# Attention and a GELU MLP on one core: the last 64 tokens of every batch gathered into one chunk, and the first batch's work reordered

## The chip, the cores and the metric

The kernel runs on one core of one Trainium2 chip. The metric is device time in microseconds (us) of one execution. A profiled execution also gives a trace: when each instruction ran on TensorE (PE, with its weight loads as PEld), VectorE (DVE), ScalarE (ACT), GpSimd (POOL) and SyncE (SP), and when each DMA was issued and landed. ACT computes the exponentials and the GELUs, POOL and SP issue the DMAs, POOL through the software queue (q0, it can change types on the way), SP through the hardware queue (q1, it can transpose).

## What is computed

Attention with a forgetting factor over 8 batches of 8 heads, 576 tokens of 64 features; then a two-layer MLP with exact GELU on the 4,608 tokens of 512 features. All inputs and the output are float32.

```python
scores = scale * q @ k.T                       # per batch and head, 576 x 576
cum    = cumsum(log(clip(f, 1e-4, 1)))         # per batch and head
scores = where(causal, -1e9, scores + cum[i] - cum[j])
attn   = softmax(scores)
x      = (attn @ v) -> 4608 x 512              # heads side by side
out    = gelu(x @ w_in) @ w_out                # 512 -> 2048 -> 512
```

The factor exp(-cum[j]) is multiplied into v (and kept as a 65th column, which gives the softmax's denominator), and exp(cum[i]) cancels, so that the kernel exponentiates the bare scores.

## The kernel before

The work of one batch is *attention(b)* and then *gemm1(b)*; *gemm2(b - 1)* is spread as filler between the matmuls of attention(b). After the last batch come gemm2(7), gemm1(8) and gemm2(8) alone.

**Attention.** Heads go in four pairs, i = 0 to 3. For a pair, `scores` (L279) computes the transposed scores, keys by queries, in four PSUM tiles t = 0 to 3, whose make-up is the list `STILES` (L27): 512, 448, 512 and 192 columns per head. ACT exponentiates each tile (L294) into an `e` tile in bf16, and POOL zeroes the part above the diagonal with `affine_select` (L296), five times in a pair. The two heads of a pair use the one `kT` tile with two query tiles, `qA` and `qB`, whose other half is zero. `attend` (L308) multiplies `e` with the weighted v, `vw`, 15 matmuls of 65 columns a head; `normalize` (L323) divides by the 65th column on DVE. A pair's 576 tokens then go to `xT_sb`, transposed: for batch 0 by PE and a DVE copy (`to_xT`, L336), later by two DMA transposes on SP (`x_dma`, L344), one for tokens 0 to 511 and one for the last 64.

**The MLP.** `xT_sb` holds all 4,608 tokens in order, and is cut into nine chunks of 512, so that chunk c begins at token 512 c and a chunk crosses batches. `gemm1(c, ffb)` (L358) is four matmuls of 512 columns and a GELU on ACT, 16 of them a chunk; `gemm2(c)` (L376) is a generator of 64 matmuls of 512 columns, each 16 followed by a DVE copy and an output DMA on SP. `take` draws so many of them between the tiles of the scores, by the lists `FILL` and `FILL_1` (L469).

**The order** is written by hand (`manual_schedule`): each engine runs its instructions in the order of the program, and each tile pool hands out its buffers in turn. Pools that matter: `qk` with one buffer (the token-major q and k of one batch), `e` with three, `s_psum`, `o_psum` and `m_psum` with two each. `m_psum` serves gemm1 and gemm2, `s_psum` the scores and some transposes.

- Batch 0 (`first_attention`, L413) has no filler. Its q and k come in four loads of two heads; PE transposes them (`transposes_first`, L169) and DVE and ACT copy them out (L183). Scores of a pair come in twos between the transposes; both heads of a pair are attended at once (`attend_pair`); DVE weighs v for pairs 0 and 2 (L269, L449), POOL for pairs 1 and 3. The four loads of w_in are issued by POOL after the pair's third scores tile (L436).
- Gemm1(0) (L517 to 527) has the PE transposes of batch 1's pairs 0, 1 and 2 in `s_psum` after ffb 10, 13 and 15 (`transposes_pe`, L194; the 8 DVE copies of each are L222) and, after ffb 2, the four loads of w_out.
- Batch 1 transposes its pair 3 within attention (L486) and then loads batch 2's q and k (L487).
- From batch 2 on, q and k of the next batch are transposed by DMA, two heads at a time, eight DMAs a batch (`transpose_dma`, L229), and put into `qA`, `qB` and `kT` by eight DVE copies a pair (`untangle`, L243) during gemm1. SP's queue before an attention holds the five loads of the next batch's v (`load_v`, L103, called at L515), then, as the attention goes on, the DMA transposes, the output DMAs and `x_dma`.

The softmax here doesn't subtract the row's maximum and nothing guards it: scores larger than these inputs give would overflow.

## Time and profile before

| | us |
|---|---|
| median of 3 runs | 377.35 (374.38 to 379.9) |
| the profiled execution's own time | 375.81 |
| its span, from the first to the last instruction | 374.1 |
| PE busy | 342.8 |
| ACT busy | 214.0 |
| DVE busy | 171.5 |
| POOL busy | 131.1 |

The span is 1.7 us shorter than the profiled execution's time. A row of the profile gives the line in the kernel, the engine, the operation, the tiles (out<-in) and the shapes; "idle before" is the time that the engine stood still just before, with what released it. The row PEclk is the clock that TensorE was granted, in tenths of the full one. A busy PE is not PE at its peak, because matmuls overlap: a matmul of 512 columns is shown with 379 ns, but one starts every 216 ns.

### The profile page before, as it was taken

To read this page: it belongs to the slowest core of one execution; us is meant where nothing else is said; L and a number is where in the kernel's file an instruction comes from. 1 tells how busy PE (TensorE), PEld (TensorE's weight loads), DVE (VectorE), ACT (ScalarE), POOL (GpSimd) and SP (SyncE) were. 2 spreads that over 40 slices of the span, in tenths; PEclk is the share of its full clock that TensorE was granted. 3 is DMA by queue.
4 is the path that set the end of the run, shared out by engine and by line. 5 is a ranking of instruction groups with operands and counts; after the bars stand their busy time and mean duration, and the time that the engine had idled before them with its cause. 6 is when DMAs were issued, how large, how long until landed. Compare 5 with 4: busy or idle time off the path is not lost.

```text
span 374.1 us, 6875 instructions
## 1 busy us (share of the span) xinstructions
PE 342.8 (92%) x2665; PEld 185.4 (50%) x2665; DVE 171.5 (46%) x420; ACT 214.0 (57%) x293; POOL 131.1 (35%) x261
## 2 busy tenths in 40 slices
PE   2858949969999699999999999999999999999995
PEld 1545526624465245644564456445654565444442
DVE  6395385548034932477246723681459142011011
ACT  4656647506874378737872688179826882611610
POOL 6578236351155404470447044703560350000000
PEclk9999978999999999999999999999999999999999
DMA  7999999767986894459644976498540023002002
GB/s 110 181 204 184 196 212 162 107 131 138 212 146 87 144 219 109 100 126 210 137 100 119 193 120 106 132 193 140 108 117 2 28 50 102 0 30 84 0 30 84
DMA packets 111057, 45.37 MB, mean 121 GB/s; under 512 B 89968, under 2 KB 106352, under 8 KB 111024
## 3 DMA queue, kind: packets, MB, share of 16 engines
q1 hardware_dynamic: 94128, 31.30, 40.7%
q0 software_dynamic: 16896, 13.63, 24.2%
q8 instruction: 21, 0.34, 0.4%
q14 instruction: 12, 0.10, 0.1%
HBM read 37.90 MB, written 9.44 MB: 127 GB/s over the span
## 4 chain that ended last, share of the span: by engine, by line
PE 77%; ACT 8%; DVE 7%; DMA 3%; SPq 2%; issue 1%; DVEq 0%; ACTq 0%
PE ps L362 33%; PE ps L394 26%; PE s L284 10%; PE o L315 7%; ACT e L294 5%; DMA xT_sb<-x 3%; ACT L294 2%; DVE vw L269 1%; ACT g L374 1%; SPq L350 1%; DVE x L329 1%; DVE ot L403 1%; DMA f_sb<-in_f_dram 1%; SPq L404 1%; DVE qB L183 1%
## 5 line engine op out<-in xcount | busy, mean ns | idle before, releaser
L374 ACT ACTIVATE g<-ps 128x512 bf16<-128x512 f32 x144 | 86.0, 597 | 111.0 <-PE ps L362 111.0
L394 PE MATMUL ps<-w_out_sb,g 128*128 128x512 bf16 x576 | 144.7, 379 | 0.0
L362 PE MATMUL ps<-xT_sb,w_in_sb 128*128 128x512 bf16 x576 | 127.2, 379 | 7.9 <-DMA xT_sb<-x 7.9
L294 ACT ACTIVATE e<-s 128x1024 bf16<-128x1024 f32 (+2 forms) x128 | 103.5, 861 | 25.5 <-PE s L284 24.9
L296 POOL TENSOR_SCALAR_AFFINE_SELECT e<-e 128x256 bf16<-128x256 bf16 x160 | 62.5, 407 | 140.0 <-ACT e L294 138.8
L362 PEld LDWEIGHTS <-w_in_sb 128*128 128x128 bf16 x576 | 56.1, 98 | 76.5 <-issue 10.3
L403 DVE COPY ot<-ps 128x512 f32<-128x512 f32 x36 | 24.9, 692 | 125.7 <-PE ps L394 124.8
L394 PEld LDWEIGHTS <-g 128*128 128x128 bf16 x576 | 50.3, 98 | 41.0
L284 PE MATMUL s<-qA,kT 128*128 128x384 bf16 (+2 forms) x192 | 54.8, 293 | 9.6 <-ACT e L294 4.2
L284 PEld LDWEIGHTS <-kT 128*128 128x128 bf16 x384 | 37.6, 100 | 46.6 <-issue 11.9
L284 PE MATMUL s<-qB,kT 128*128 128x384 bf16 (+2 forms) x192 | 50.3, 294 | 0.3 <-DVE qB L183 0.3
L269 POOL TENSOR_TENSOR vw<-v,wT 128x640 bf16<-128x640 f32 x30 | 38.8, 1292 | 27.6 <-PE o L315 18.5
L315 PE MATMUL o<-vw,e 128*128 128x65 bf16 x960 | 43.6, 194 | 1.6 <-DVE vw L275 1.4
L315 PEld LDWEIGHTS <-e 128*128 128x128 bf16 x960 | 40.4, 98 | 9.1 <-issue 1.4
L328 DVE RECIPROCAL r<-o 128x5 f32<-128x5 f32 x64 | 12.4, 193 | 48.0 <-PE o L315 47.1
L252 DVE COPY kT<-tk 64x288 bf16<-64x288 bf16 x96 | 32.2, 336 | 1.4
L329 DVE TENSOR_TENSOR x<-o,r 128x320 bf16<-128x320 f32 x64 | 31.5, 492 | 2.2
L252 DVE COPY qA<-tq 64x288 bf16<-64x288 bf16 x48 | 20.8, 433 | 0.9
L252 DVE COPY qB<-tq 64x288 bf16<-64x288 bf16 x48 | 16.7, 348 | 0.7
L98 POOL DMA_DIRECT2D q<-in_q_dram x12 | 9.1, 756 | 9.0 <-DMA tq<-q 7.9
L294 ACT ACT_TABLE_LOAD x7 | 9.0, 1283 | 3.3 <-PE s L284 3.2
L374 ACT ACT_TABLE_LOAD x8 | 10.3, 1283 | 0.1
(52 smaller groups left out, 88.5 us busy)
## 6 DMA issues: line engine op xcount, KB each, us to landing
out_dram<-ot SPq DMA_DIRECT2D x36, 256.0 KB, 2.3
v<-in_v_dram SPq DMA_DIRECT2D x30, 256.0 KB, 9.3
q<-in_q_dram POOLq DMA_DIRECT2D x6, 576.0 KB, 7.5
k<-in_k_dram POOLq DMA_DIRECT2D x6, 576.0 KB, 10.7
v<-in_v_dram SPq DMA_DIRECT2D x20, 128.0 KB, 5.3
w_in_sb<-in_moe_w_in_dram POOLq DMA_DIRECT2D x4, 512.0 KB, 10.2
w_out_sb<-in_moe_w_out_dram POOLq DMA_DIRECT2D x4, 512.0 KB, 13.6
xT_sb<-x SPq DMA_TRANSPOSE x56, 2.4
```

What stands on the lines that cost most here:

```text
L252: nc.vector.tensor_copy(rows[:, odd], src[odd * D : (odd + 1) * D, 2 * i + h].rearrange("d j p -> d p j"),)
L269: eng.tensor_tensor(vw_of[b][:, hs, :, 0:D], v_of[b][:, hs, :, :], w.unsqueeze(3).to_broadcast([P, 2, NBLK, D]), Alu.mult,)
L284: nc.tensor.matmul(st[:, h, c : c + w], kT[i][:, K0[n] : K0[n] + P], qt[:, q0 : q0 + w], start=True, stop=True,)
L294: nc.scalar.activation(et[:, :, 0:c], st[:, :, 0:c], Act.Exp, scale=scale)
L296: nc.gpsimd.affine_select(out=et[:, :, c0 : c0 + P], in_=et[:, :, c0 : c0 + P], compare_op=Alu.is_ge, fill=0.0, base=0, pattern=[[0, 2], [ ...
L315: nc.tensor.matmul(o[:, m, :], e_of[b, i, t][:, h, c : c + P], vw_of[b][:, 2 * i + h, n, :], start=(n == 0), stop=(n == m),)
L328: nc.vector.reciprocal(r, o[:, :, D])
L329: nc.vector.tensor_tensor(x_of[b, i][:, :, h, :], o[:, :, 0:D], r.unsqueeze(2).to_broadcast([P, NBLK, D]), Alu.mult,)
L362: nc.tensor.matmul(ps, w_in_sb[:, kt, ffb * P : (ffb + 1) * P], xT_sb[:, kt, t0 : t0 + TC], start=(kt == 0), stop=(kt == n_dm - 1),)
L374: nc.scalar.activation(g_of[c][ffb], ps, Act.Gelu)
L394: nc.tensor.matmul(pss[ts], g_of[c][kt][:, ts * P : (ts + 1) * P], w_out_sb[:, kt, :], start=(kt == 0), stop=(kt == n_ff - 1),)
L403: nc.vector.tensor_copy(ot, pss[ts])
```

## The change

1. **Chunks.** Chunk b is now the first 512 tokens of batch b, and the ninth chunk is the last 64 tokens of all eight batches. `xT_sb` gives way to a tile `xT` a batch (two buffers) and a tile `tails`. `normalize` writes tokens 0 to 511 and the tail separately, one more small instruction a head (on ACT for pairs 2 and 3 of batch 0, else on DVE). `x_dma` is one DMA transpose a pair, and `x_tail_dma` one a batch, so that a batch has five in place of eight. The last 128 output rows of all are made in a part of 384 columns and one of 128.
2. **Transposes of q and k by DMA** take four heads each, four a batch in place of eight, in attention(b) at pair 0 and pair 1. The `qk` pool has two buffers.
3. **Loads of v** go into one fixed tile `v_sb`, the last block with 64 rows in place of 128; from batch 2 on they are issued within attention(b), after its second scores tile, behind two DMA transposes.
4. **Score tiles** are balanced: 448, 448, 448 and 320 columns per head. `e` has four buffers.
5. **Batch 0.** A matmul of the identity with a tile `after` (0 and -1e9) adds the mask in PSUM in place of POOL's `affine_select`. Scores of later pairs come ahead, and the heads of earlier pairs are attended between them. POOL weighs all four pairs of v. Two of the four copies to `xT` go to ACT. Nine matmuls on a zeroed tile (`warm_up`) come first, and four more after the first transposes. On POOL the loads of w_in, the weighing and the loads of batch 1 alternate; batch 1's v is loaded in there too.
6. **Batches 0 and 1.** The transposes of batch 1's pairs 0 and 1 come in gemm1(0) after ffb 6 and 8, those of pairs 2 and 3 in attention(1). The four loads of w_out and batch 2's q and k are issued before gemm1(0). v of batch 1 is weighed for pairs 0 and 1 after ffb 9 and 10, for pairs 2 and 3 in attention(1) at pair 2.
7. **Fillers at the end of an attention**: the lists end in 8, 0, 20 in place of 8, 4, 16, and 8, 0, 99 in place of 8, 4, 99.

```diff
 STILES = [
-    [(0, 0, 384), (4, 448, 128)],
+    [(0, 0, 256), (3, 384, 192)],
+    [(0, 256, 320), (4, 448, 128)],
     [(1, 128, 448)],
-    [(2, 256, 320), (0, 384, 192)],
-    [(3, 384, 192)],
+    [(2, 256, 320)],
 ]
...
-    qk_pool = ctx.enter_context(tc.tile_pool(name="qk", bufs=1))
+    qk_pool = ctx.enter_context(tc.tile_pool(name="qk", bufs=2))
-    e_pool = ctx.enter_context(tc.tile_pool(name="e", bufs=3))
+    e_pool = ctx.enter_context(tc.tile_pool(name="e", bufs=4))
+    xT_pool = ctx.enter_context(tc.tile_pool(name="xT", bufs=2))
...
+    def warm_up(n):
+        ps = m_psum.tile([P, TC], FP32, tag="m", name="ps_w")
+        for _ in range(n):
+            nc.tensor.matmul(ps, warm[:, 0:P], warm, start=True, stop=True)
...
-    def transpose_dma(b, i):
+    def transpose_dma(b, h0, h1):
...
     def scores(b, i, t):
...
-                    stop=True,
+                    stop=b > 0 or c not in SDIAG[t],
                 )
+            if b == 0 and c in SDIAG[t]:
+                for h in range(2):
+                    nc.tensor.matmul(
+                        st[:, h, c : c + P], ident_bf, after, start=False, stop=True
+                    )
...
-        for c0 in SDIAG[t]:
+        for c0 in SDIAG[t] if b else []:
...
     def normalize(b, i, h):
...
-            o[:, :, 0:D],
-            r.unsqueeze(2).to_broadcast([P, NBLK, D]),
+            o[:, 0:4, 0:D],
+            r[:, 0:4].unsqueeze(2).to_broadcast([P, NBLK - 1, D]),
...
+        tail = xt_of[b][D:P, i, h, :], o[D:P, 4, 0:D]
+        if b == 0 and i > 1:
+            nc.scalar.mul(*tail, r[D:P, 4:5])
+        else:
+            nc.vector.tensor_scalar(*tail, r[D:P, 4:5], None, Alu.mult)
...
     def x_dma(b, i):
-        x, q0 = x_of[b, i], b * S
         nc.sync.dma_start_transpose(
-            xT_sb[:, i, q0 : q0 + 512].rearrange("d (m p) -> d m p", p=P),
-            x[:, 0:4].rearrange("p m h d -> p (m h d)"),
+            xT(b)[:, i, :].rearrange("d (m p) -> d m p", p=P),
+            x_of[b, i].rearrange("p m h d -> p (m h d)"),
         )
+
+    def x_tail_dma(b):
         nc.sync.dma_start_transpose(
-            xT_sb[:, i, q0 + 512 : q0 + S].unsqueeze(1),
-            x[D:P, 4].rearrange("p h d -> p (h d)"),
+            tails[:, :, b * TL : (b + 1) * TL],
+            xt_of[b][D:P].rearrange("p i h d -> p (i h d)"),
         )
...
     def gemm1(c, ffb):
-        t0 = c * TC
+        src = xT(c) if c < B else tails
...
     def first_attention():
...
+        warm_up(9)
         transposes(0, o_psum, "o")
+        zero_halves(range(2, HP))
+        warm_up(4)
         scores(0, 0, 0)
+        transposes(1, m_psum, "m")
         scores(0, 0, 1)
...
+        scores(0, 1, 3)
+        weigh_v(0, 0)
+        load_w_in(0)
+        load_w_in(1)
+        weigh_v(0, 1)
+        load_qk_tokens(1, 0, 4)
+        weigh_v(0, 2)
+        weigh_v(0, 3)
+        load_w_in(2)
+        load_w_in(3)
+        nc.gpsimd.memset(v_sb[:, :, 0, 0:1], 0.0)
+        load_v(1, 0, 4)
+        load_v(1, 4, 8)
+        load_qk_tokens(1, 4, 8)
         scores(0, 2, 0)
+        attend_head(0, 0)
         scores(0, 2, 1)
+        attend_head(0, 1)
         scores(0, 2, 2)
         scores(0, 2, 3)
+        attend_head(1, 0)
         scores(0, 3, 0)
+        attend_head(1, 1)
+        to_xT(0, 0, nc.vector.tensor_copy)
         scores(0, 3, 1)
         scores(0, 3, 2)
+        attend_head(2, 0)
         scores(0, 3, 3)
+        attend_head(2, 1)
+        to_xT(0, 1, nc.scalar.copy)
+        attend_head(3, 0)
+        attend_head(3, 1)
+        to_xT(0, 2, nc.scalar.copy)
+        to_xT(0, 3, nc.vector.tensor_copy)
...
-    FILL = [[4, 6, 2, 2], [2, 2, 2, 2], [2, 2, 2, 2], [2, 2, 1, 1], [8, 4, 16]]
-    FILL_1 = [[0, 0, 0, 0], [2, 2, 2, 2], [2, 2, 2, 2], [2, 2, 2, 2], [8, 4, 99]]
+    FILL = [[4, 6, 2, 2], [2, 2, 2, 2], [2, 2, 2, 2], [2, 2, 1, 1], [8, 0, 20]]
+    FILL_1 = [[0, 0, 0, 0], [2, 2, 2, 2], [2, 2, 2, 2], [2, 2, 2, 2], [8, 0, 99]]
...
     def attention(b, fill, counts):
...
-                if b == 1 and i == 0 and t == 2:
-                    transposes_pe(1, 3, in_s=False)
-                    load_qk_tokens(2)
...
+                if t == 0 and b > 1 and i < 2:
+                    transpose_dma(b + 1, 4 * i, 4 * i + 4)
+                if t == 1 and i == 0 and b > 1:
+                    load_v(b + 1)
+                if b == 1 and (i, t) in ((0, 0), (0, 3)):
+                    transposes_pe(1, 2 + t // 3, o_psum)
+                if b == 1 and i == 2 and t in (0, 2):
+                    weigh_v(1, 2 + t // 2)
                 take(fill, counts[i][t])
...
         x_dma(b, i)
+        x_tail_dma(b)
         if b == 1:
-            transpose_dma(2, 3)
+            transpose_dma(2, 0, 4)
+            transpose_dma(2, 4, 8)
+            load_v(2)
         take(fill, 999)
 
     for b in range(B):
         if b == 0:
             first_attention()
-            load_v(1, 0, 4)
-            load_v(1, 4, 8)
         else:
-            load_v(b + 1)
             attention(b, gemm2(b - 1, b == 1), FILL_1 if b == 1 else FILL)
+        if b == 0:
+            for c in range(4):
+                load_w_out(c)
+            load_qk_tokens(2)
+            x_tail_dma(0)
         for ffb in range(n_ff):
             gemm1(b, ffb)
...
+            if b == 0:
+                if ffb in (6, 8):
+                    transposes_pe(1, ffb // 2 - 3, s_psum)
+                if ffb in (9, 10):
+                    weigh_v(1, ffb - 9)
...
+                if ffb == 14:
+                    load_qk_tokens(b + 2)
```

## The prediction

> **What bounds the kernel now.** I read the page's busy rows and slices first, then the table of stretches, the chain of waits, and the timelines of ACT, PE and SP where the table shows idle PE.
>
> ```profile
> PE 342.8 (92%) x2665; PEld 185.4 (50%) x2665; DVE 171.5 (46%) x420; ACT 214.0 (57%) x293; POOL 131.1 (35%) x261
> PE   2858949969999699999999999999999999999995
> PEclk9999978999999999999999999999999999999999
> ```
>
> PE bounds the kernel: from slice 8 on it hardly stops. What can be won is its idle time, 31.3 us, and that lies mostly in the first 125 us. Table of stretches (length; busy time of PE, PEld, DVE, ACT, POOL; clock, DMA):
>
> ```profile
> 0.00:33.40 33.40, 20.07 (x290) 14.66 (x291) 23.77 (x47) 19.45 (x23) 23.47 (x49) 1.00 0.98 167
> 33.40:51.50 18.10, 15.45 (x102) 7.75 (x101) 8.19 (x18) 9.55 (x16) 9.01 (x13) 1.00 1.25 197
> 51.50:84.80 33.30, 27.17 (x248) 16.07 (x249) 19.23 (x48) 15.74 (x18) 14.94 (x30) 0.90 0.83 143
> 98.70:125.70 27.00, 23.79 (x231) 13.94 (x229) 11.20 (x26) 15.48 (x19) 15.03 (x30) 1.00 0.77 135
> 139.70:163.00 23.30, 23.11 (x229) 13.83 (x228) 7.63 (x20) 15.43 (x18) 11.39 (x25) 1.00 0.51 108
> 328.80:370.40 41.60, 41.55 (x193) 18.55 (x190) 4.85 (x8) 10.15 (x17) 0.00 (x0) 1.00 0.12 45
> ```
>
> The reader sees PE idle 13.3 us in batch 0's attention, 2.7 about gemm1(0), 6.1 in batch 1, 3.2 in batch 2, and almost nothing in an undisturbed batch. In the first stretch ACT is the longest dependent chain, and it waits for scores between its bursts:
>
> ```profile
> 9.78 1.83 ACT L294 ACTIVATE e<-s 128x1024 bf16<-128x1024 f32 x2 [2.15 <-PE s L284]
> 24.17 1.41 ACT L294 ACTIVATE e<-s 128x1024 bf16<-128x1024 f32 x2 [2.28 <-PE s L284]
> 27.20 3.17 ACT L294 ACTIVATE e<-s 128x1024 bf16<-128x1024 f32 x4 [1.63 <-PE s L284]
> ```
>
> Next, PE waits for DVE's copies after gemm1(0), and for the DMA of x after attention(1), while SP has worked without a break since 62.81:
>
> ```profile
> 51.47 0.34 PE L284 MATMUL s<-qA,kT 128*128 128x384 bf16 x1 [2.65 <-DVE kT L222]
> 80.36 0.81 PE L362 MATMUL ps<-xT_sb,w_in_sb 128*128 128x512 bf16 x3
> 84.77 1.46 PE L362 MATMUL ps<-xT_sb,w_in_sb 128*128 128x512 bf16 x6 [3.60 <-DMA xT_sb<-x]
> ```
>
> ```profile
> 78.35 1.27 SPq L238 DMA_TRANSPOSE tq<-q  x1
> 79.67 1.27 SPq L238 DMA_TRANSPOSE tk<-k  x1
> 81.04 1.00 SPq L404 DMA_DIRECT2D out_dram<-ot  x2
> 82.13 1.22 SPq L346 DMA_TRANSPOSE xT_sb<-x  x1
> ```
>
> Measured from GELU end to GELU end in the chain, batches 2 to 6 take 40.9, 37.7, 38.3, 38.5 and 37.7 us. 37.65 is the undisturbed period.
>
> **What stays.** The number and columns of the gemm matmuls (nine chunks) and of the scores (1,664 a head and pair) are the same, so the period of 37.65 and the last 41.5 us of matmuls (328.84 to 370.37) stay. ACT's work a pair too: 2 x 1.02 + 0.91 + 0.49 = 3.44 us before, 3 x 0.91 + 0.70 (320 columns, between the rows of 0.49 and 0.91) after. The tail's multiply (eight a batch, 0.23 each by DVE's 64x64 copy) lies under PE, since DVE has 7 to 12 us of work in a 23 us attention; without that cover it would cost 1.8 a batch.
>
> **Step 1, batch 0 (gemm1(0) begins at 33.4).** DVE now copies kT before it zeroes the other halves, so qB is out at 7.9 in place of 9.0; 13 warm-up matmuls (0.43 each at half clock) fill PE from 1.4 to 5.3, before k lands at 5.58, and to 7.8 or 8.7. The first exponential begins at 8.9 (8.5 to 10.0). All 16 are 13.8 us. Mask matmuls: 40 of 128 columns at 0.055 to 0.11, 2.2 to 4.4 us of PE beside ACT. They free POOL of 20 selects (0.41 each, 8.1 us), and DVE loses two weighings (1.95 + 0.73 each). POOL now weighs all four: the first when v has landed (15.2, as before), 1.5 each (1.29 + 0.22), with four DMA issues of 0.75 between: 15.2, 18.2, 21.2, 22.7, done at 24.2. Pair 1 attended at 19.7 holds the next scores back some 0.5, and the second and third scores tiles behind transposes cost ACT 0.8 more. ACT also gets two multiplies (0.25 each) and ends at 24.6; then two heads (0.47 each), normalize (0.20 + 0.41, twice), four transposes and the copy (0.35 + 0.45): gemm1(0) at 27.2. Low end, no hole in ACT: 25.5. High end: POOL's small cast took 0.84 and 0.82 beside DVE's weighing, 0.22 to 0.28 otherwise; I take 0.22, since DVE's weighing is gone, but with 0.84 four times and a cold PE it is 30. **Minus 6.2 (minus 7.9 to minus 3.4).**
>
> w_in must land by then: before, its four loads took 15 us from first issue to last landing. Now two are issued at 16.7, landing at 22 to 24; batch 1's q and k (first half) by 27, the other two by 34, due at 27.2 + 7 and + 10.4. Covered, by little for the third.
>
> **Step 2, gemm1(0).** 16 x 0.867 + 2 x 0.51 for transposes = 14.9, against 18.07 to the first scores at 51.47: one group of transposes fewer, and the copies (3.9 us a pair) of both done before the end. **Minus 3.2.** If they were not, the 2.65 returns.
>
> **Step 3, attention(1).** Before 28.9 (51.47 to 80.36), of which 6.9 until the first filler. New is that pairs 2 and 3 are transposed here in `o_psum`, whose two buffers wait for DVE: pair 3's k cannot start before 5 us, so the next scores come at 5.4 and ACT idles 0.7. Then PE has three pairs of scores, eight heads and 64 fillers, 22.2 us: 27.6. Bounds: 25 (only PE's work, 23.8, and the table load of 1.28), 31.5 (v of batch 1, issued at 25 beside the weight loads. There q1 moved 0.04 MB/us before; 1.2 MB then land at about 54, and POOL wants them at 53). **Minus 1.3 (minus 3.9 to plus 2.6).**
>
> **Step 4, x of batch 1.** SP had 8 transposes of q and k and 8 of x before the gemm, about 1.27 and 1.23 each. Now the q and k transposes stand behind x, and x needs one DMA. From the last head: 0.65 + 1.23 + 1.2 to land = 3.1, under 32 fillers of 0.216 (6.9). **Minus 3.6.**
>
> **Step 5, batch 2.** Queue: v(2) now stands behind batch 2's transposes and is issued as gemm1(1) begins; it lands 8.2 later, POOL weighs for 6 us, and only then issues q and k of batch 3, whose loads take 6.0 and 9.3. SP meets their transposes first in attention(2): it waits till 10.4 us into it, then v (4.8), two transposes, outputs and four of x: the last lands at 26.3, where PE is ready at 23.75 and has 0.65 of work without it. Stall 1.9 to 2.5 in place of 3.3. **Minus 0.9 (minus 3.3 to plus 1.5).**
>
> **Step 6, batches 3 to 7.** SP had 8 x 1.27 + 8 x 1.23 + 4 x 0.52 + 10.4 to 12.4 (v) = 32.5 to 34.5 us of work in 37.65; that lateness is the 0.6 and 0.9 lost in batches 4 and 5. Now 4 x 1.3 + 5 x 1.23 + 2.1 + 4.8 to 12.4 = 18 to 26. A transpose of one block took 1.22 and of six 1.27, so I take 1.3 for twelve; its bound is 2.5. v is issued when no q and k load runs (alone: 4.8 on SP). 20 fillers (4.3) cover the last x's 3.1. **Minus 1.5 (to plus 6).**
>
> **Step 7, end.** The last copy is 128 columns: 0.25 for 0.69, and its DMA 64 KB for 256; 16 matmuls more cost 0.05. **Minus 0.5 (minus 0.8 to plus 0.3).**
>
> Sum: 6.2 + 3.2 + 1.3 + 3.6 + 0.9 + 1.5 + 0.5 = 17.2; span 356.9, profiled time 358.6. The profiled execution stood 1.5 under the median of the runs, so the median: **360**.
>
> **The clock.** In the trace, matmuls of 448 columns start 0.37 apart at 9.54 and 0.19 apart at 19.86: half clock first, full from about 17.7. It fell again from 52.05 to 58.88 (the 0.90 above), after PE had idled 2.65. I take full clock from about 7. The Trainium skill, "TensorE: Matmul & The Clock Gate", Part 1, says that one busy window of about 3.4 us lifts the gate, which the warm-up would meet. Its Part 4 says transposes do not count as busy in the same way, which speaks against the change: with 24 transposes between the warm-ups the clock would rise only with the scores. By Part 1 the sum stands; by Part 4 it is 1.2 us more. No run here separates them.
>
> **The rivals.**
> *Loads collide in the first 60 us.* For it: DMA is already near its limit there (0.98 and 1.25 of share), and POOL's queue mixes weighing with issuing. Against it: no more bytes, and none due earlier than my landings. Steps 1 and 3 then give back 5: 365.
> *The clock does not hold.* Cold batch 0 (the first two tiles of scores and a group of transposes at half speed: 0.6 + 0.5 + 0.5, less 0.4 under ACT: 1.2) and a half clock in attention(1), where fillers are still 0 for a pair (7 us at half speed, half of it behind ACT, 3.4): 364.6.
> *SP becomes the bound: slower.* v now stands ahead of x within an attention. If its issue takes 12.4 us there as well, and twelve blocks take 2.5: q and k transposes until 3.3, v 15.7, two more 20.7, outputs 1.0 and x 4.9: 26.6, landed at 27.9, against 24.4 needed: 3.4 in each of six batches, less the 2.3 already counted in batch 2: plus 18, 378. It decides from 2.9 us a batch. Against it: v alone took 4.8.
> *Fewer stalls still* (batch 2 none, ACT without holes): 356.
>
> **How the numbers follow.** My forecast 0.60 (own range 357 to 363), loads 0.14, clock 0.10, fewer stalls 0.11, SP 0.05. The range 354 to 368 leaves out SP and the worst of the loads. A measurement here tells about 2%, 7.5 us, from no change: faster is below 369.8. All but SP and a part of the loads (0.04, with more than 5 given back) lie there: 0.91; same 0.07, which takes that part and 0.03 of SP's 0.05; slower 0.02, where SP costs 4.2 a batch or more.
>
> **What would show it.** Gemm1(0)'s first matmul at 27 with ACT's exponentials nearly unbroken from 9; first scores of batch 1 some 15 us later without a wait on a copy; no wait on the DMA of x after attention(1), one of about 2 after attention(2), none later; periods of 37.65; v's five issues in 5 us of SP. Wrong if PE's idle time returns at the start of batch 1, if x is waited for in every batch, or if the period itself grows.

## The result and the profile after

The changed kernel takes 389.77 us (median of 4 runs, 388.09 to 391.0), the kernel before beside it 376.42 (374.38 to 379.9). The ratio is 1.034, with a 95% interval of 1.025 to 1.043: slower by 3.4%, where 360.0 was forecast. The profiled execution took 390.52, its span 388.8. The four executions span 386.4 to 389.3, so that spans less than about 3 us apart say little by themselves, and the stages are read instead.

The page of the changed kernel shows PE busier than before only in sum; three dips stand out: in slices 6 and 12 (counted from 0) and at the end.

```profile
PE 346.9 (89%) x2684; PEld 189.4 (49%) x2730; DVE 177.4 (46%) x478; ACT 216.9 (56%) x298; POOL 124.9 (32%) x248
...
PE   7989795999981799999999999999999999999940
...
PEclk9999998999997599999999999999999999999985
```

The table of stretches of the changed kernel, cut where its stages begin (length; busy time and count of PE, PEld, DVE, ACT, POOL; granted clock, DMA share, GB/s):

```profile
0.00:27.40 27.40, 22.67 (x339) 16.20 (x340) 21.14 (x49) 20.23 (x28) 19.94 (x39) 1.00 1.00 158
27.40:42.40 15.00, 14.87 (x87) 7.25 (x89) 7.67 (x16) 10.17 (x16) 3.05 (x4) 1.00 1.23 193
42.40:77.00 34.60, 26.91 (x252) 16.15 (x256) 16.95 (x43) 16.35 (x19) 13.01 (x28) 0.95 0.86 133
...
115.40:128.40 13.00, 1.42 (x4) 0.43 (x5) 9.98 (x29) 0.00 (x0) 5.83 (x10) 0.70 0.97 171
128.40:144.50 16.10, 16.05 (x61) 6.72 (x62) 3.35 (x11) 8.96 (x15) 0.00 (x0) 0.81 0.98 190
144.50:331.60 187.10, 185.62 (x1454) 102.63 (x1481) 94.52 (x268) 125.89 (x170) 67.07 (x138) 1.00 0.53 102
...
373.90:388.80 14.90, 0.00 (x0) 0.00 (x0) 0.03 (x1) 0.00 (x0) 0.00 (x0) 0.59 0.12 45
```

The first two rows and the long row of batches 3 to 7 are as good as forecast or better. The third has 7.7 us of idle PE, the fourth 11.6 of 13, and in the last no engine works for 14.9 us, while DMA moves 45 GB/s at a share of 0.12, about 2 of 16 engines.

Set side by side, with each stage from the end of the one above, that is from the end of its last matmul or of the wait behind it (us; "fixed" is the version of the experiments in which three costs are taken away):

| stage | before | forecast | changed | fixed |
|---|---|---|---|---|
| to the first matmul of gemm1(0) | 33.3 | 27.2 | 27.4 | 27.6 |
| gemm1(0), with the wait behind it | 18.1 | 14.9 | 15.2 | 15.2 |
| attention(1) | 28.9 | 27.6 | 34.5 | 29.9 |
| gemm1(1), attention(2), gemm1(2) | 58.7 | 54.2 | 67.6 | 51.4 |
| batches 3 to 7 | 189.8 | 188.3 | 187.1 | 187.1 |
| from there to the end | 45.3 | 44.8 | 57.1 | 46.7 |
| span | 374.1 | 356.9 | 388.8 | 357.9 |

So 31.9 us are missing against the forecast. They lie in three places, 6.9 in attention(1), 13.4 about batch 2 and 12.3 at the end; the other stages together are 0.7 better than forecast.

**Attention(1) and batch 2.** PE's timeline in the changed kernel (start, length; in brackets the idle time before and who ended it):

```profile
60.84 0.22 PE L343 MATMUL o<-vw,e 128*128 128x65 bf16 x2 [2.50 <-POOL vw L298]
61.53 0.27 PE L343 MATMUL o<-vw,e 128*128 128x65 bf16 x3 [0.47 <-POOL e L324]
63.27 0.24 PE L343 MATMUL o<-vw,e 128*128 128x65 bf16 x1 [1.48 <-POOL e L324]
...
120.44 0.79 PE L403 MATMUL ps<-xT,w_in_sb 128*128 128x512 bf16 x2 [5.06 <-DVE ot L450]
122.29 0.59 PE L403 MATMUL ps<-xT,w_in_sb 128*128 128x512 bf16 x1 [1.06 <-DMA xT<-x]
128.36 16.28 PE L403 MATMUL ps<-xT,w_in_sb 128*128 128x512 bf16 x60 [5.48 <-DMA xT<-x]
```

In attention(1) PE waits for POOL, which weighs v and has its selects queued behind that. In batch 2 it waits three times at the head of gemm1(2), and when it goes on at 128.4 the clock is half until 134.4: 60 matmuls take 16.28. The releaser of the first of these waits, an output copy of DVE, is itself held: DVE stood 7.1 us before it, in `normalize`, for a buffer of x that a DMA had still to read. POOL's timeline names what it waited for itself:

```profile
59.34 1.28 POOL L292 TENSOR_TENSOR vw<-v_sb,wT 128x640 bf16<-128x640 f32 x1 [4.05 <-DMA v_sb<-in_v_dram]
...
60.71 0.77 POOL L324 TENSOR_SCALAR_AFFINE_SELECT e<-e 128x256 bf16<-128x256 bf16 x2
...
88.78 1.28 POOL L292 TENSOR_TENSOR vw<-v_sb,wT 128x640 bf16<-128x640 f32 x1 [20.89 <-DMA v_sb<-in_v_dram]
...
94.26 0.81 POOL L102 DMA_DIRECT2D q<-in_q_dram  x1
95.07 0.77 POOL L102 DMA_DIRECT2D k<-in_k_dram  x1
```

Both times it is v. The second time the loads of batch 3's q and k stand behind the weighing. SP's timeline shows what follows from that, queue entry after queue entry (start, time to issue):

```profile
103.67 2.43 SPq L262 DMA_TRANSPOSE tk<-k  x1
106.20 4.35 SPq L114 DMA_DIRECT2D v_sb<-in_v_dram  x5
110.59 2.28 SPq L262 DMA_TRANSPOSE tq<-q  x1
112.91 1.37 SPq L262 DMA_TRANSPOSE tk<-k  x1
...
115.40 2.53 SPq L385 DMA_TRANSPOSE xT<-x  x2
...
118.66 3.46 SPq L385 DMA_TRANSPOSE xT<-x  x2
```

SP could not pass `tk<-k` before k landed, and everything else of attention(2) stood behind it, x last. The chain of waits has the flights themselves (start and length):

```profile
44.71 14.46 DMA v_sb<-in_v_dram
...
84.23 4.38 DMA v_sb<-in_v_dram
...
115.40 2.43 DMA xT<-x
120.41 7.91 DMA xT<-x
```

Two transposes of x, 512 tokens of one pair each: one lands 2.43 after its issue, the other 7.91. The second was issued 0.8 us after POOL had issued the load of batch 4's q (119.65, landing at 126.95). The experiments are about these three places, and about what the right parts of the forecast rest on.

### The profile page after: what moved, and what is told of

Same layout as the page of the kernel before. It is cut to its first block, busy times and chain, and to the rows that moved or that the text cites. A ratio compares the mean times of both kernels' runs of the same rounds, so it can differ in the third digit from the quotient of the medians.

```text
span 388.8 us, 6967 instructions
## 1 busy us (share of the span) xinstructions
PE 346.9 (89%) x2684; PEld 189.4 (49%) x2730; DVE 177.4 (46%) x478; ACT 216.9 (56%) x298; POOL 124.9 (32%) x248
## 4 chain that ended last, share of the span: by engine, by line
PE 66%; SPq 12%; DMA 8%; POOL 6%; issue 2%; DVE 1%; ACT 0%; POOLq 0%; DVEq 0%; ACTq 0%
PE ps L441 26%; PE ps L403 26%; SPq L114 9%; PE s L307 8%; DMA v_sb<-in_v_dram 6%; PE o L343 6%; POOL vw L292 3%; DMA xT<-x 3%; SPq L262 3%; POOL k L102 1%; POOL e L324 1%; POOL q L102 1%; DVE x L359 0%; POOL w_in_sb L160 0%; DVE ot L450 0%
## 5 line engine op out<-in xcount | busy, mean ns | idle before, releaser
L441 PE MATMUL ps<-w_out_sb,g 128*128 128x512 bf16 (+2 forms) x557 | 138.7, 374 | 1.6
L403 PE MATMUL ps<-xT,w_in_sb 128*128 128x512 bf16 x503 | 115.9, 387 | 12.7 <-DMA xT<-x 6.5
L322 ACT ACTIVATE e<-s 128x896 bf16<-128x896 f32 (+1 forms) x128 | 104.8, 863 | 24.2 <-PE s L307 17.7
L450 DVE COPY ot<-ps 128x512 f32<-128x512 f32 (+2 forms) x37 | 25.0, 677 | 121.6 <-PE ps L441 121.4
L441 PEld LDWEIGHTS <-g 128*128 128x128 bf16 x592 | 52.4, 98 | 42.5
L292 POOL TENSOR_TENSOR vw<-v_sb,wT 128x640 bf16<-128x640 f32 x32 | 40.8, 1276 | 55.1 <-DMA v_sb<-in_v_dram 46.2
L307 PE MATMUL s<-qA,kT 128*128 128x256 bf16 (+2 forms) x192 | 51.8, 282 | 2.7 <-ACT e L322 2.4
L307 PE MATMUL s<-qB,kT 128*128 128x256 bf16 (+2 forms) x192 | 48.5, 282 | 0.5 <-DVE qB L206 0.5
L359 DVE TENSOR_TENSOR x<-o,r 128x256 bf16<-128x256 f32 x64 | 27.2, 425 | 9.3 <-DMA xT<-x 7.1
L369 DVE TENSOR_SCALAR xt<-o,r 64x64 bf16<-64x64 f32 x60 | 17.5, 291 | 1.4
L403 PE MATMUL ps<-tails,w_in_sb 128*128 128x512 bf16 x62 | 14.2, 378 | 0.1
```

The costliest lines, as they stand in the source:

```text
L292: nc.gpsimd.tensor_tensor(vw_of[b][:, hs, :, 0:D], v_sb[:, hs, :, :], w.unsqueeze(3).to_broadcast([P, 2, NBLK, D]), Alu.mult,)
L307: nc.tensor.matmul(st[:, h, c : c + w], kT[i][:, K0[n] : K0[n] + P], qt[:, q0 : q0 + w], start=True, stop=b > 0 or c not in SDIAG[t],)
L322: nc.scalar.activation(et[:, :, 0:c], st[:, :, 0:c], Act.Exp, scale=scale)
L359: nc.vector.tensor_tensor(x_of[b, i][:, :, h, :], o[:, 0:4, 0:D], r[:, 0:4].unsqueeze(2).to_broadcast([P, NBLK - 1, D]), Alu.mult,)
L403: nc.tensor.matmul(ps, w_in_sb[:, kt, ffb * P : (ffb + 1) * P], src[:, kt, :], start=(kt == 0), stop=(kt == n_dm - 1),)
L441: nc.tensor.matmul(pss[ts][:, c0:c1], g_of[c][kt][:, ts * P : (ts + 1) * P], w_out_sb[:, kt, c0:c1], start=(kt == 0), stop=(kt == n_ff - 1),)
```

## The experiments

Spans are compared, one execution each, unless a ratio is given.

**The end: one output DMA a batch** (`tail_by_batch`). The rows of the last chunk belong to two batches of 64 in each 128. The changed kernel writes them as one DMA of shape 2x64x512.

```diff
-                    rows = out.rearrange("(b s) d -> b s d", s=S)[
-                        n * ts : n * (ts + 1), TC:S, c0:c1
-                    ]
+                    for j in range(P // TL):
+                        r0 = (P // TL * ts + j) * S + TC
+                        nc.sync.dma_start(
+                            out[r0 : r0 + TL, c0:c1], ot[j * TL : (j + 1) * TL, c0:c1]
+                        )
+                    yield
+                    continue
```

> Each output DMA of the last chunk (two batches of 64 rows, 2x64x512) is cut into two of 64 rows, one a batch; the last 128 rows stay cut into 384 and 128 columns. Theory A, a DMA whose outermost dimension is 2 runs on two of the 16 DMA engines: after the last matmul the changed kernel needed 15.2 us, with a DMA share of 0.12, that is 2 of 16. With 64 rows outermost the end comes 3 to 4 us after the last matmul, and the span falls by 11 to 12 us, from 388.8 to 377. Rival B, the short rows of the column parts (1,536 and 512 bytes) are what is slow: they are unchanged here, so the span stays at 387 to 389. Rival C, the number of stores in the queue: there are more of them, so it stays or grows.

Span 376.2, 12.6 less. The stretch from the last matmul to the end, in this kernel:

```profile
371.40:376.20 4.80, 0.01 (x1) 0.00 (x0) 0.29 (x1) 0.00 (x0) 0.00 (x0) 1.00 0.22 55
```

4.8 us in place of 15.2. The other 2.2 of the difference lie in attention(1) (0.8 shorter) and batch 2 (1.4), which this edit doesn't touch.

**The end: no split of columns** (`tail_whole_cols`), with the output still written as 2x64x512.

```diff
-        if c == B:
-            order[-n_ff:] = [
-                (n_sub - 1, kt, part)
-                for part in ((0, 3 * P), (3 * P, d_model))
-                for kt in range(n_ff)
-            ]
```

> The last 128 rows are made whole, 512 columns and one DMA; the DMAs of the last chunk keep the two batches outermost. Theory A (two engines): the bytes and the engines are as before, so the end comes as late, span 388 to 390. Rival B (short rows): 10 us less, 378.

The end takes 15.0 us after the last matmul, again at a share of 0.12. So the shape of the DMA is the cost, and the split in columns neither costs nor brings anything that can be seen there. The span is 385.2, 3.6 less and under the 388 to 390 expected, but not at the end: attention(1) took 31.5 in place of 34.5 and batch 2 1.6 less, while gemm1(0) began 1.2 later. The edit touches none of these, so two executions can differ by that much there.

**Batch 2: the load of q and k earlier** (`qk3_early`): the load of batch 3's q and k at ffb 0 of gemm1(1), ahead of the weighing, in place of ffb 14.

```diff
+                if b == 1 and ffb == 0:
+                    load_qk_tokens(3)
...
-                if ffb == 14:
+                if ffb == 14 and b > 1:
```

> In gemm1(1) POOL issues the loads of batch 3's q and k before it weighs batch 2's v, not after. Theory: batch 2's stall of 13 us before gemm1(2) (115.4 to 128.4) comes from POOL waiting until 88.6 for v, so that k of batch 3 landed at 103.6, and SP, whose queue has its transpose first, fell 10 us behind; x of the last pair was then issued at 120.4, into the loads of batch 4, and landed 7.9 us later. With the loads out by 78 the transposes run when attention(2) begins; gemm1(2) follows without a stall over 1 us, the half clock of 120.7 to 134.4 is gone, and the span falls by 13 to 15 us, to 374 to 376. Rival: the transposes of twelve blocks (2.3 us on SP at 110.6 and 199) and the new place of v keep SP late whatever k does: a stall of 5 us or more stays.

From the end of gemm1(1) to gemm1(2) it is 23.4 us in place of 29.4, and gemm1(2) takes 14.0 at full clock in place of 24.2: batch 2's stall is gone. But gemm1(1) now takes 20.3 in place of 14.0. POOL had nothing to do and issued the loads at 66.9, still within attention(1). PE's timeline:

```profile
75.93 0.81 PE L403 MATMUL ps<-xT,w_in_sb 128*128 128x512 bf16 x3
80.20 16.01 PE L403 MATMUL ps<-xT,w_in_sb 128*128 128x512 bf16 x61 [3.46 <-DMA xT<-x]
```

and the flight that it waited for, in the chain of waits:

```profile
70.47 9.70 DMA xT<-x
```

The stall has moved to the x of batch 1: span 377.8, 10.9 less, of which 16 come from batch 2 and 6 are given back here; 374 to 376 was expected.

**Attention(1): a second tile for v** (`v1_second_tile`), so that batch 1's v needn't wait for the weighing of batch 0's, and is issued right after the first two loads of w_in.

```diff
-    v_sb = consts.tile([P, H, NBLK, D], FP32)
+    v_sb = [consts.tile([P, H, NBLK, D], FP32, name=f"v_sb{i}") for i in range(2)]
...
         load_w_in(1)
+        nc.gpsimd.memset(v_sb[1][:, :, 0, 0:1], 0.0)
+        load_v(1, 0, 4)
+        load_v(1, 4, 8)
         weigh_v(0, 1)
...
```

> v has two tiles in turn, and batch 1's v is issued by SP after the first two loads of w_in (about 17.5 us) in place of 24.7, since it need not wait for batch 0's weighing. Theory: attention(1)'s 34.6 us against 27.6 forecast come from the second half of batch 1's v, which landed at 59.2 behind the loads of weights, while POOL's selects queue behind the weighing. Landed by 50, attention(1) takes 27.5 to 29 us and the span falls by 6 to 7, to 382 to 383; gemm1(0) may lose up to 1.5 where w_in lands later. Rival: the wait for o_psum and the copies of pairs 2 and 3, and the half clock from 62.7, set attention(1): it stays above 32 us.

The rows of gemm1(0) and attention(1):

```profile
27.60:44.30 16.70, 16.69 (x90) 7.86 (x90) 7.69 (x16) 10.22 (x16) 5.99 (x9) 0.90 1.24 195
44.30:73.40 29.10, 26.48 (x257) 16.25 (x256) 16.93 (x43) 16.46 (x19) 10.51 (x24) 0.94 0.90 147
```

Attention(1) takes 29.1 in place of 34.5, and no PE instruction waits for a weighing. The span falls by 3.7, not the 6 to 7 expected, because gemm1(0) had 3.4 us of half clock (0.90 in its row) and cost 1.5 more. Why the clock fell there is open; in the 3.4 us before it PE was busy for 1.8.

**The three together** (`all_fixed`): the second tile for v, the output by batches (both edits as above), and the load of batch 3's q and k behind the last weighing of attention(1), where v is there already.

```diff
                 if b == 1 and i == 2 and t in (0, 2):
                     weigh_v(1, 2 + t // 2)
+                    if t == 2:
+                        load_qk_tokens(3)
...
-                if ffb == 14:
+                if ffb == 14 and b > 1:
```

> The changed kernel with the three named costs taken away together: v of batch 1 goes to a second tile and is issued before the scores of batch 0's second half; the last rows go out as one DMA of 64 rows a batch; the load of batch 3's q and k is issued in attention(1), after the last weighing, and no longer in gemm1(1). Theory (three separate costs, each a transfer): attention(1) takes 29 us in place of 34.65, gemm1(1) stays at 14, gemm1(2) follows 23 to 24 us after the end of gemm1(1) and runs at full clock, the last output lands 4.8 us after the last matmul; span 388.8 less 10.4 (end), less 4 to 6 (attention(1), after the 1.5 that gemm1(0) gives back), less 13 to 15 (batch 2): 358 to 362, time 360 to 364, under the kernel before by 3 to 4%. Rival (the loads of batch 3 only collide elsewhere, as they did with x when they were issued at the start of gemm1(1)): the DMA of x after attention(1) lands some 8 us late and gemm1(1) takes 20 again; span 365 to 368. Rival (the costs are not independent; DMA traffic of the first 120 us is simply too much for the time it has): span 370 or more.

359.66 us (median of 4 runs), the kernel before beside it 377.23: a ratio of 0.954, 95% interval 0.950 to 0.958. The span is 357.9, just under the 358 to 362 expected. Its table from attention(1) on:

```profile
42.80:72.70 29.90, 24.73 (x251) 15.30 (x255) 16.93 (x43) 16.36 (x19) 12.04 (x26) 1.00 1.25 193
72.70:86.70 14.00, 13.95 (x66) 6.39 (x66) 11.10 (x33) 8.96 (x15) 2.35 (x3) 1.00 1.08 204
86.70:110.10 23.40, 23.13 (x229) 14.16 (x232) 9.36 (x27) 16.23 (x19) 15.19 (x32) 1.00 0.74 139
110.10:124.10 14.00, 13.95 (x66) 6.36 (x66) 11.85 (x33) 8.96 (x15) 3.21 (x6) 1.00 0.80 145
124.10:311.20 187.10, 185.61 (x1454) 102.63 (x1480) 94.48 (x268) 125.91 (x170) 67.19 (x138) 1.00 0.59 113
311.20:353.10 41.90, 41.68 (x205) 19.48 (x206) 5.40 (x8) 10.16 (x17) 0.00 (x0) 1.00 0.15 44
353.10:357.90 4.80, 0.00 (x0) 0.00 (x0) 0.29 (x1) 0.00 (x0) 0.00 (x0) 0.77 0.23 55
```

The three costs were independent enough to be taken away together: no stretch after attention(1) has more than 0.3 us of idle PE till the last matmul but for the 1.5 in the five batches. The clock is full from 4.1 until after the last matmul. This version is faster than both kernels. Attention(1) still has one wait of 2.3, for a select that stands on POOL behind the weighing and, from 58.27 to 59.85, behind the issuing of batch 3's q and k.

**The late flight by itself** (`qk4_late`). The changed kernel, in which POOL copies one element of gemm1(2)'s first output before it loads batch 4's q and k, so that this load can't fly beside x.

```diff
+    probe = consts.tile([P, 1], BF16)
...
                 if ffb == 14:
+                    if b == 2:
+                        nc.gpsimd.tensor_copy(probe, g_of[b][0][:, 0:1])
                     load_qk_tokens(b + 2)
```

> The changed kernel, but the load of batch 4's q and k waits (one element copied by POOL) for the first GELU of gemm1(2), so that it can't be in flight beside x of batch 2. Theory (a DMA transpose that meets a load of q and k in flight lands some 6 to 8 us late): the fourth transpose of x, issued at 120.4 as before, lands at 122 to 123 in place of 128.3, the next 5.5 us of idle PE and most of the half clock that follows are gone, and gemm1(2) ends at 137 to 139 in place of 144.6; the 5.06 us before gemm1(2) stay, since they come from x being issued late. Span 381 to 383. Rival (the fourth transpose is late for what stands ahead of it on SP's own queue, the five loads of v and the output): it still lands at about 128 and the span stays 387 to 389.

The chain of waits and PE's timeline of this kernel:

```profile
122.63 2.65 DMA xT<-x
```

```profile
122.61 1.00 PE L404 MATMUL ps<-xT,w_in_sb 128*128 128x512 bf16 x2 [4.84 <-DVE ot L451]
124.48 0.58 PE L404 MATMUL ps<-xT,w_in_sb 128*128 128x512 bf16 x1 [0.88 <-DMA xT<-x]
125.33 15.36 PE L404 MATMUL ps<-xT,w_in_sb 128*128 128x512 bf16 x61 [0.26 <-DMA xT<-x]
```

The same transpose behind the same queue flies 2.65 us in place of 7.91; the wait of 5.48 becomes 0.26, and the wait of 5 before it stays. The rival (SP's own queue ahead of it) is out. The sizes are smaller than I expected: the span is 384.8, 4.0 less, not 6 to 8. From its first matmul on gemm1(2) takes 6.1 less (18.1 for 24.2). But gemm1(0) began 1.2 later in this run, x was issued 2.2 later, and after 4.84 us of idle PE the clock was halved all the same, for 6.8 us in place of 13.7.

**Transposes of two heads** (`two_head_transposes`): eight DMAs a batch for q and k in place of four.

```diff
-        for src, dst in zip(qk_of[b], tq_of[b]):
-            nc.sync.dma_start_transpose(
-                dst[:, h0:h1].rearrange("d h j p -> d (h j) p"),
-                src[:, h0:h1].rearrange("p h c -> p (h c)"),
-            )
+        for g in range(h0, h1, 2):
+            for src, dst in zip(qk_of[b], tq_of[b]):
+                nc.sync.dma_start_transpose(
+                    dst[:, g : g + 2].rearrange("d h j p -> d (h j) p"),
+                    src[:, g : g + 2].rearrange("p h c -> p (h c)"),
+                )
```

> The changed kernel with the DMA transposes of q and k of two heads each, as before: eight a batch, at the same places. SP then has some 4 x 1.27 = 5 us more to issue in a batch. Theory (SP has room once v takes 4.8 and x five DMAs): batches 3 to 7 keep their period, 37.4 to 37.6, and batch 2 is as late as in the changed kernel or up to 3 us later; span 388 to 393. Rival (the four-head transposes are what gained the 0.25 us a batch, or SP is near its limit): period 38 or more, span 392 to 400.

Span 398.1, 9.4 more. Batches 3 to 7 keep 187.1 us exactly, so SP is no bound there. Batch 2 is 8 us later, where I had expected 3 at most: v of batch 2 stands behind eight transposes and is weighed from 93.38 on, then the loads (98.87) and all that SP has behind them move along, and x meets batch 4's load again. Its last flight in the chain of waits:

```profile
128.14 10.88 DMA xT<-x
```

So here fewer transposes helped where SP was late, in batch 2, and nowhere else. The span lies in the rival's range, but not for the rival's reason, since the period is unchanged.

**No warm-up** (`no_warm_up`): the changed kernel without the 9 + 4 matmuls on zeros.

```diff
-        warm_up(9)
...
-        warm_up(4)
```

> The changed kernel without its 13 warm-up matmuls. If they are what lifted the clock at 4.7 us, the first group of transposes and the first scores run at half clock, full clock comes some 7 us or more after 4.7, and gemm1(0) begins 0.6 to 1.2 us later than 27.4, at 28.0 to 28.6. If ACT's chain covers it, the clock rises late but gemm1(0) still begins at 27.4 to 27.6. If the transposes lift the clock as well as matmuls do, full clock comes within 3.4 to 6.8 us of the first transpose (5.6), by 12.4 at the latest.

The clock was full from 16.2 us, not 4.7, and gemm1(0) began at 31.06: 3.7 us later, three times what I had put on it. The second q and k also landed 1.7 us later than in the changed kernel (10.01 for 8.34), so not all of the 3.7 need be the clock. But the span is 387.5, which is 1.3 *less* and within the spread of the changed kernel. The table from the first transpose on:

```profile
5.80:10.60 4.80, 3.38 (x44) 2.67 (x46) 3.00 (x7) 2.35 (x4) 2.48 (x8) 1.00 1.18 174
10.60:16.20 5.60, 5.60 (x61) 3.96 (x57) 3.19 (x6) 2.61 (x4) 0.80 (x1) 1.00 0.91 188
...
46.20:76.90 30.70, 26.33 (x252) 16.31 (x255) 16.94 (x43) 16.46 (x19) 13.35 (x28) 0.94 0.89 134
```

(The clock column doesn't show the cold start as less than 1.00; that the clock was half is read from the matmuls: a transpose group of ten takes 0.70 in place of 0.47.) Attention(1) takes 30.7 in place of 34.5: it ends at 76.9 for 77.0, though gemm1(0) ended at 46.2 for 42.5. In the seven kernels here that keep v of batch 1 in the one tile it ended at 75.2 to 77.8, in no order with the end of gemm1(0). In all seven POOL waited for v before it weighed pair 2 of batch 1, at 58.9 to 60.6; in the four kernels with the second tile it did not wait there, and weighed at 54.8 to 57.0. What batch 0 won, attention(1) gave back.

**The three together, no warm-up** (`fixed_no_warm_up`), the same two lines taken out of `all_fixed`.

> The kernel with the three costs taken away, without its 13 warm-up matmuls. In the changed kernel they moved gemm1(0) by 3.7 us but the span by 1.3. Theory (there attention(1) waited for v of batch 1, which lands at the same time either way, and gave back the rest): with v in a second tile more of the 3.7 reaches the end: gemm1(0) at 31.0 to 31.4, span 360.4 to 361.6 (357.9 + 2.5 to 3.7). Rival (what follows batch 0 is limited by the transfers of w_in, w_out and of q and k here too): span 358.5 to 359.5.

Gemm1(0) begins at 29.81, 2.2 later than with the warm-up, less than the 3.4 to 3.8 that I expected, and gemm1(1) (74.95 for 72.74), every later stage and the end (360.1 for 357.9) are 2.2 later too. So here all of it reaches the end, which is the theory; the size between the two ranges comes from the smaller shift at the start. Here full clock came at 13.8, and the second q and k landed as with the warm-up (8.62).

**The old score tiles** (`old_tiles`): `all_fixed` with the lists `STILES` and `SDIAG` of before (`SDIAG` names where the diagonal lies in each tile).

```diff
 STILES = [
-    [(0, 0, 256), (3, 384, 192)],
-    [(0, 256, 320), (4, 448, 128)],
-    [(1, 128, 448)],
-    [(2, 256, 320)],
+    [(0, 0, 384), (4, 448, 128)],
+    [(1, 128, 448)],
+    [(2, 256, 320), (0, 384, 192)],
+    [(3, 384, 192)],
 ]
...
```

> The kernel with the three costs taken away, with the score tiles of before (512, 448, 512 and 192 columns per head in place of 448, 448, 448 and 320). Batches 3 to 7 took 37.42 us with the new tiles; before with only the chunks changed 37.67. Theory (the balanced tiles are what is left of that difference): period 37.6 to 37.7, five periods 1.2 us longer, batch 0 up to 1 us longer; span 359.3 to 360.5. Rival (the last fillers or the transposes of four heads are): period 37.4 to 37.45, span 357.5 to 359.

The period is 37.67 in place of 37.42 and the span 359.6, 1.7 more, 0.4 of it in batch 0. The waits of the weight loads from batch 3 to the last scores show where (waited, times, longest); first the old tiles, then the new ones:

```profile
PEld L308 <- issue: 3.8, 10, 0.4
```

```profile
PEld L308 <- issue: 2.5, 10, 0.3
```

1.3 us in five batches, about the quarter of a microsecond a batch. Why the loads wait longer at the old tiles was not tried.

**Only the chunks** (`chunks_only`): the kernel before with part 1 of the change alone, except that the last rows are written by batches of 64, without a split of columns, and that DVE multiplies all the tails.

```diff
-                xT_sb[:, kt, t0 : t0 + TC],
+                src[:, kt, :],
...
-            xT_sb[:, i, q0 + 512 : q0 + S].unsqueeze(1),
-            x[D:P, 4].rearrange("p h d -> p (h d)"),
+            tails[:, :, b * TL : (b + 1) * TL],
+            xt_of[b][D:P].rearrange("p i h d -> p (i h d)"),
...
```

> The kernel before with the chunks of the changed one alone (tails of all batches as ninth chunk, one x transpose a pair and one a batch, last rows out as one DMA of 64 rows a batch). Theory (the merged transposes of x are worth the wait after attention(1) and part of the later ones): the 3.60 us wait of gemm1(1) is gone or under 1, batch 2's 3.3 shrinks to 1 to 3, the 0.6 and 0.9 of batches 4 and 5 are gone, and the end costs 4.8 for 3.7: span 374.1 - 3.6 - 1 - 1.5 + 1.1 = 369 (366 to 371). Rival (the wait is not SP's count of DMAs but what the transposes of x meet in flight): the waits stay within 1 us and the span is 373 to 376.

Span 370.6, 3.5 under the profiled kernel before, within the range. The wait of 3.60 on x after attention(1) is 0.9, that of gemm1(2) is gone (14.2 from its first matmul to its last, for 17.3), and batches 3 to 7 take 37.67 us each. In return gemm1(0) begins at 35.9, 2.6 later; DVE's busy time there is 25.4 for 23.8, and the clock was full only from 24.5, in the trace of before from 17.9. What each is worth is not shown.

## Why the prediction was wrong, point by point

**Steps 1 and 2 held.** Gemm1(0) began at 27.4 for the 27.2 forecast and took 15.2 for 14.9, without a wait on a copy behind it. The first exponential began at 9.0 for 8.9, POOL's casts took 0.22 to 0.24, the clock was full from 4.7. What was mis-sized inside is the warm-up: I counted 1.2 us for a cold start, and without it gemm1(0) was 2.2 and 3.7 later. The early clock was also luck in part. Nine traces here have the same nine matmuls, from 1.26 to about 5. In six the clock was full from 3.9 to 6.2 and gemm1(0) began at 27.4 to 28.0; in `tail_whole_cols`, `qk3_early` and `qk4_late` it was full only from 10.0 to 10.6, and gemm1(0) began at 28.5 to 28.7. The first transposes show it, in the changed kernel and in `qk4_late`:

```profile
5.77 0.47 PE L198 MATMUL ps_f<-ident_bf,k 96*64 96x96 bf16 x10 [0.73 <-DMA k<-in_k_dram]
```

```profile
5.79 0.70 PE L199 MATMUL ps_f<-ident_bf,k 96*64 96x96 bf16 x10 [0.51 <-DMA k<-in_k_dram]
```

On the clock, the Trainium skill's "TensorE: Matmul & The Clock Gate", Part 1, has one busy window of about 3.4 us lift it; in the changed kernel's trace the nine warm-up matmuls (1.26 to 5.04) with full clock from 4.7 agree, while in the three traces just named as many did not suffice. Its Part 4, that transposes do not count as busy in the same way, isn't refuted: without the warm-up the stretch of 5.8 to 10.6 with its transposes did not lift the clock, and that of 10.6 to 16.2, where PE never stopped, did. But PE was busy for only 3.38 of 4.80 in the first, so no run here separates the kind of work from its density.

**Step 3 failed in its size**, by 6.9 us. Its upper bound named the mechanism ("v of batch 1, issued at 25 beside the weight loads ... land at about 54, and POOL wants them at 53"), and the value taken in the end, minus 1.3, left it out. v landed at 59.2: its 1.2 MB took 34.5 us from the first issue, 0.034 MB/us, where the bound went by 0.04. SP had issued its second half between 30.6 and 45.5, and it flew beside q0's weights, whose last landed at 51.9, and q and k of batch 2, the last at 61.4. The upper bound of 31.5 was itself too low, since it had v one us late and no clock: POOL's wait delays its selects as well, and the clock was halved for 3.4 us after. The second tile shows it: 29.1 and 29.9. The last 2.3 above 27.6 hold the one wait of 2.3 for a select.

**Step 4 held**: gemm1(1) takes 14.0 us without a wait on x. `chunks_only` shows that the merged transposes alone nearly do it.

**Step 5 is the one that failed in its mechanism**, by 13.4 us. It forecast the order of the queues rightly: v, weighing, loads, SP's wait, x. It forecast the last x to land 26.3 us into attention(2); it landed at 37.3, 11.0 later, and its issue and its flight have half of that each. By the step's own terms (1.23 to issue, 1.2 more to land) the issue would begin at 23.9; it began at 29.4. Of these 5.5, 2.2 came from k, landing 12.6 us into the stage for 10.4, and 2.1 from two transposes of 2.4 and 2.3 where I took 1.3 and kept 2.5 as the bound; the rest are small gaps between SP's entries, the longest, 0.5, before the last x. The other half is what the step did not contain: it priced x's flight as a free one, 2.4 from the begin of its issue, while the change issues the next load of q and k in just that moment, and the flight took 7.9. PE, idle meanwhile, came back at half clock, so that what followed of gemm1(2) took 16.1 where the step has 13.9. `qk4_late` and `qk3_early` show the flight to be the load's doing. The trace of before had the price: there a transpose issued at 124.50, 0.3 us after a load of q, landed 6.6 us later, at 131.12, where the median of its line is 2.4 (min/median/max):

```profile
124.50 1.22 SPq L350 DMA_TRANSPOSE xT_sb<-x  x1
...
DMA to landing us min/median/max: 2.3/2.4/6.6
```

**Step 6 was right in sign and small in size**: batches 3 to 7 won 2.7 us, not 1.5. 37.67 is what the merged transposes of x reach by themselves (`chunks_only`), and 1.25 in five batches are from the balanced tiles, which I had costed at nothing because ACT's time for a pair is the same. The time shows on PE's side, in the weight loads of the scores. v took about 4.8 us of SP there, so the rival in which SP becomes the bound did not come.

**Step 7 failed outright**, by 12.3 us, and needed no run to be seen. Its "and its DMA 64 KB for 256" prices an output DMA by its bytes. The changed one has another shape, 2x64x512, and moved 45 GB/s on a DMA share of 0.12. The Trainium skill states the rule, in "DMA: Bandwidth & Descriptors", section "Why a DMA increments its semaphore by 16 and not by 1", under "How many engines": the transfer is spread over the largest number up to 16 that divides the outermost dimension of both sides, here 2. The trace agrees: 2 of 16 is 0.125, measured 0.12, and with 64 rows outermost the same bytes end 4.8 us after the last matmul in place of 15.2. The gain of 0.5 doesn't come even so: before, the end took 3.8 after the last matmul, and `chunks_only`, with 64 rows and whole columns, took 4.6.

**The rivals.** "Loads collide in the first 60 us" was nearest to what came, but at 5 us it was priced too low, and it ended where attention(1) ended; the same collision 60 us later was in no case. Slower had been given 0.02, and for SP as the bound of every batch, which it was not. With the three costs gone the kernel's span is 357.9 for the 356.9 forecast. That the sums agree so well is partly luck: attention(1) is 2.3 and the end 1.9 over the forecast, batch 2, without any stall, 2.8 and batches 3 to 7 1.2 under it.

## What to carry to other kernels

Price a DMA by its shape and by what flies beside it, not by its bytes: look at the outermost dimension on both sides, and for each load that a change moves list the transfers that it will now meet. A gain ahead of a stage that waits for a transfer doesn't reach the end; here 3.7 us won in batch 0 brought nothing that the span shows, and 2.2 of 2.2 arrived once the transfer was early. When a large change turns out slower, take its costs away one by one before the idea is dropped: three edits of a few lines made 389.8 into 359.7.

## What the runs showed of the hardware

- A DMA transpose of x on SP lands about when the q and k load of the software queue lands that it meets. Of the transposes whose landing the thirteen traces tell, 27 were issued while such a load still had over 4 us to go. They landed 5.0 to 10.9 us after their issue, and all but one within 1.5 us of the landing of the load. The 239 that met no load took 2.3 to 4.7 us, with a median of 2.4.
- Within a run the changes of the clock lie whole multiples of 3.41 us apart; the half clock came in stretches of 3.4, 6.8, 10.2, 13.7 and 17.1 us. The first change does not keep to the kernel's start: in the nine traces with warm-up matmuls, from 1.26 on in each, it came between 3.9 and 10.6. After the 5.1 and 5.5 us waits of batch 2 the half clock lasted from 120.7 to 134.4, though PE ran without a break from 128.4 on.
- Issuing a DMA on SP had no fixed price: one transpose of twelve blocks took 1.3 to 2.4 us in the changed kernel and up to 3.6 in `qk3_early`, and the five loads of v 4.4 to 4.9 us from batch 2 on in the changed kernel, 10.4 to 12.4 in the kernel before.
